# A GEGLU feed-forward block on one core: two raw products of the second column unit moved into the first one's second half, and the load queue of the down projection re-ordered

## The chip, the core and the metric

The kernel runs on one core of a Trainium2 chip. The metric is the device time in microseconds (us) of one execution; the lower, the better. Engines are named as in the profile: PE is the matrix engine, DVE the vector engine, ACT the scalar engine, POOL the GpSimd engine, SP the sync engine, which here only issues DMA transfers.

## What is computed

```python
B, S, Dm, Df = 1, 2048, 1024, 3584          # everything bf16
g = jnp.einsum("bsd,df->bsf", x, w_gate)
u = jnp.einsum("bsd,df->bsf", x, w_up)
h = jax.nn.gelu(g, approximate=True) * u
return jnp.einsum("bsf,fd->bsd", h, w_down)
```

## The kernel before

The 2048 rows of x are worked in two passes of 1024, each as two halves of 512 rows, `xT[0]` and `xT[1]`, held transposed. In a pass, the gate and up products come first, then the down projection.

**The gate and up products.** The 3584 hidden columns are cut into 14 units of 256 columns, each with one weight tile `w` of 2 x 512 KB (gate and up) from a pool of three buffers. A unit treats its product as a 2x2 block product and computes it in seven block products instead of eight, with sums of weight blocks (`s1` to `s4`, and `sa`, a cast) and sums of x blocks (`t1` to `t4`, and `tb`, a cast). The x sums serve the whole pass; a unit's weight sums are made a unit ahead on POOL. Each block product is 4 matmuls of 128x128 by 512 columns, and gate and up have one each, so a unit has 7 x 2 x 4 = 56 matmuls. Two of the seven use raw bf16 operands: `first_product` (L188), which needs only the weights' first half and `xT[0]`, and the product with `b21` at the head of `unit` (L205). The five others use the sums, in fp32r. A unit's order on PE is: `b21` product, s2 t2, s1 t1, s3 t3, s4 tb, then the next unit's `first_product`, then sa t4. Between s1 t1 and s3 t3 stands the call `after_p5()`, which is `prepare()` (L520): it makes the next unit's sums and issues loads.

Unit 0 of pass 0 is different: it has no sums and runs as plain products (`plain`, L471) of 32 matmuls for each half of x (a few of them cut in two). `xT[0]` is turned on PE. `xT[1]` comes by eight transposing DMAs on SP (L448), one for each block `ko` of 128 columns of x; the second half of unit 0 takes the blocks `ko` in order, two at a time.

**The down projection** (`down`, L361) is one large block product of the same kind with 14 column pairs j and a hand-written agenda. A step is a number in that agenda; on each step the functions due are called in the order they were entered, then `more(step)`, then the matmuls. Steps 0 to 27 use w_down as it is: 14 tiles `raw` of 256 KB, fetched by `fetch12`, each used by two steps of 4 matmuls. Then three stages follow that use sums of w_down blocks. Those sums are made in pass 0 (`keep_part`, `keep_whole`), stored to a DRAM tile `td` (`store_made`, L279, 768 KB each), and loaded again by `load12` (L286; for j = 0, 2 and 4 two at a time in 1 MB, with a buffer of the weight pool) and `load4` in both passes.

**What sets the order.** SP, DVE, POOL and PE run in the program's order throughout (`manual_schedule` with these engines). ACT is ordered by the compiler's own scheduler, except in blocks that add ACT to the list: the start with unit 0, and in unit 1 the snaps and the gelu after s2 t2. Small tiles come from one pool of 52 slots; an instruction that takes a slot waits for its last reader, and on SP everything behind it waits too. Weights of unit 1 and 2 are issued from ACT's queue, all later ones from SP's.

Of the kernel before, what the change touches and what calls it, by code (L numbers as in the profile page):

```python
# [1 line left out]

# [8 lines left out]
def kernel(  # L11
# [23 lines left out]
    nc = tc.nc  # L35
    ENG = mybir.EngineType
# [7 lines left out]
    ADD, SUB, MUL = ALU.add, ALU.subtract, ALU.mult  # L44
# [6 lines left out]
    NKB = Dm // P  # L51
# [8 lines left out]
    SLOTS = 52  # L60
    LAG = 3
    BIG12 = (0, 2, 4)
    AT12 = [2, 2, 5, 5, 8, 8, 16, 18, 20, 22, 27, 29, 31, 33]
    AT12S = [2 * j + (j > 8) for j in range(NJ)]
    AT73 = [30 + 2 * j if j < 8 else 46 + j - 8 for j in range(NJ)]

# [28 lines left out]
    def new(eng, a, b, op, name, shape=None, dtype=None):  # L95
        t = slot(shape or [P, N], dtype or f32r, name)
        eng(t, a, b, op)
        return t
# [6 lines left out]
    def snap(ps, name):  # L105
        t = slot([P, N], f32, name)
        nc.scalar.copy(out=t, in_=ps)  # L107
        return t
# [5 lines left out]

    def load_w(u, queue=nc.sync, pinned=False):
        f0 = u * 2 * P
        w = wpool.tile([P, 2, NKB, 2 * P], bf16, name="w")
        for i, src in enumerate((w_gate, w_up)):  # L120
            got = queue.dma_start(
                out=w[:, i],
                in_=src[:, f0 : f0 + 2 * P].rearrange("(ko ki) f -> ki ko f", ki=P),
            )
            if queue is not nc.sync and not pinned:
                tc.keep_in_program_order(got)
        return w

    class Sums(dict):
# [6 lines left out]
    def sums_t(xT):  # L136
        K = range(KH)
        lo, hi = [[xT[c][:, k] for k in K] for c in range(2)], [
            [xT[c][:, KH + k] for k in K] for c in range(2)
        ]  # L140
        return Sums(
            how={
                "t1": lambda q: [new(dve, lo[1][k], lo[0][k], SUB, "t1") for k in K],
                "t2": lambda q: [new(dve, hi[1][k], q["t1"][k], SUB, "t2") for k in K],
                "t3": lambda q: [new(dve, hi[1][k], lo[1][k], SUB, "t3") for k in K],
                "t4": lambda q: [new(dve, hi[0][k], q["t2"][k], SUB, "t4") for k in K],
                "tb": lambda q: [cast(hi[1][k], "tb") for k in K],
            }
        )
# [26 lines left out]
    def gelu(src):  # L176
        g = slot([P, N], f32, "g")
        nc.scalar.activation(g, src, ACT.Gelu_apprx_tanh)  # L178
        return g
# [4 lines left out]
    def product(ps, lhs, rhs, start):  # L184
        for k in range(KH):
            matmul(ps, lhs[:, k, :], rhs[k], start and k == 0, k == KH - 1)
# [6 lines left out]
    def unit(u, banks, xT, w, s, t, p1, after_p5, aside, keep, ahead_of_p4, snap_first):  # L193
        GU = range(2)

        def add(ps, other):

            g = new(dve, ps[0], other[0], ADD, "sum", dtype=f32)
            dve(ps[1], ps[1], other[1], ADD)
            return g, ps[1]  # L200

        b21 = [xT[0][:, KH + k, :] for k in range(KH)]
        e, c, d = banks
        aside(-1)
        for i in GU:  # L205
            product(c[i], w[:, i, KH:, :P], b21, True)
        g, up = add(c, p1)
        for i in GU:
            product(e[i], s["s2"][i], t["t2"], False)
        aside(0)  # L210
        keep(0, c[0])
        if snap_first:
            with tc.manual_schedule(engines={ENG.Activation}):
                u2 = [snap(e[i], "u2") for i in GU]
                g = gelu(g)
        else:
            g = gelu(g)
        times(2 * u, 0, g, up)
        if not snap_first:
            u2 = [snap(e[i], "u2") for i in GU]  # L220
        keep(1, c[0])
        keep(2, c[1])
        c = d
        for i in GU:
            product(c[i], s["s1"][i], t["t1"], True)
        p5 = [snap(c[i], "p5") for i in GU]
        after_p5()
        for i in GU:
            product(e[i], s["s3"][i], t["t3"], False)
        g, up = new(dve, e[0], p5[0], ADD, "sum", dtype=f32), banks[1][1]  # L230
        dve(up, e[1], p5[1], ADD)
        for i in GU:
            product(c[i], s["s4"][i], t["tb"], False)
        times(2 * u + 1, 1, gelu(g), up)
        aside(1)
        g, up = add(c, u2)
        ahead_of_p4()
        for i in GU:
            product(e[i], s["sa"][i], t["t4"], False)
        times(2 * u, 1, gelu(g), up)  # L240
        aside(2)
        times(2 * u + 1, 0, gelu(e[0]), e[1])
# [36 lines left out]
    def store_made(j):  # L279
        nc.sync.dma_start(out=td[:, j], in_=made[j][:, :3].bitcast(f32))  # L280
# [55 lines left out]
    def at(step, what, j):  # L336
        agenda.setdefault(int(step), []).append((what, j))

    for n in range(NJ):
        at(max(-1, 2 * n - 6), fetch12, n)  # L340
    for j in range(NJ):
        at(AT12[j], load12, j)
        at(AT12S[j], make12, j)
# [121 lines left out]
    wf = wpool.tile([P, 2, NKB, 2 * P], bf16, name="w")  # L465
    for k0, k1 in ((0, 2), (2, 5), (5, NKB)):
        load_wf(nc.sync, k0, k1)
    for ko in range(NKB):
        transposing(xT, 1, ko, N)

    def plain(ps, c, kos, parts=1):  # L471
# [14 lines left out]
    def finish(ps, c):  # L486
        for j in range(2):
            times(j, c, gelu(ps[2 * j]), ps[2 * j + 1])

    on_dve, on_act = nc.vector.tensor_copy, nc.scalar.copy  # L490
    t = sums_t(xT)
    with tc.manual_schedule(engines={ENG.Activation}):
        for _ in range(NWARM):
            nc.tensor.matmul(bank[3], lhsT=warm[:, :P], rhs=warm, start=True, stop=True)
        for i in range(NS):
            turn(xT, xn0, 0, i, on_act if i == 1 else on_dve)
        w = load_w(1, nc.scalar, pinned=True)
        s = sums_s(w, dve)
        plain(bank[0:4], 0, range(0, 2), parts=2)
        plain(bank[0:4], 0, range(2, NKB))  # L500
        t.make("t1")
        finish(bank[0:4], 0)
        s.make("s1", "s2")
        t.make("t2", "t3", "tb")
        s.make("s3", "sa")
        plain(bank[4:8], 1, range(NKB))
        finish(bank[4:8], 1)

    def making(u):
        if u < 2 or u >= NU:  # L510
            return []
        return list(range(u - 2, NJ if u == NU - 1 else u - 1))

    nxt = {}
    ahead = None
    for ip in range(NPASS):
        for u in range(1 if ip == 0 else 0, NU):
            js = making(u) if ip == 0 else []

            def prepare():  # L520
                nonlocal ahead
                nxt["w"], nxt["s"] = ahead, None
                if u + 1 < NU:
                    nxt["s"] = make_s(ahead, pool)
                if u + 2 < NU:
                    ahead = load_w(u + 2)
                if js:
                    store_made(js[0])
                for j in js[1:]:
                    keep_whole(j)  # L530
                if ip == 0:
                    fetch_wd(making(u + 1))

            def keep(part, ps):
                if js:
                    keep_part(js[0], part, ps)

            def aside(part):
                nonlocal ahead
                if ahead is None:  # L540
                    ahead = load_w(2, nc.scalar)
                if part == 0 and "s4" not in s:
                    s.make("s4")
                    t.make("t4")

            def ahead_of_p4():
                if u + 1 < NU:
                    nxt["p1"] = first_product(even if u % 2 else odd, xT, nxt["w"])

            e = odd if u % 2 else even  # L550
            p1 = nxt.pop("p1", None) or first_product(e, xT, w)
            unit(u, (e, cc, dd), xT, w, s, t, p1, prepare, aside, keep, ahead_of_p4, ip == 0 and u == 1)
            if u + 1 < NU:
                w, s = nxt["w"], nxt["s"]

        last = ip == NPASS - 1
        got, nxt = {}, {}

        def more(step):

            nonlocal ahead
            if last:
                return
            if step in (-1, 1):
                store_made(NJ - 2 + (step > 0))
            if step == 0:
                xT[:] = new_x()
            if step >= 16 and step % 2 == 0 and step // 2 - 8 < len(moves):
                c, ko = moves[step // 2 - 8]
                transposing(xT, c, ko, (2 * (ip + 1) + c) * N)  # L570
            if step == 50:
                got["w"], ahead = load_w(0), load_w(1)
            if step == 58:
                got["s"] = make_s(got["w"], dve)
            if step == 62:
                got["t"] = make_t(xT)

        down(ip, even + cc, dd + odd, last, more)
        even, odd, cc, dd = odd, even, dd, cc
        if not last:  # L580
            w, t, s = got["w"], got["t"], got["s"]
# [29 lines left out]
```

## Time and profile before

| | us |
|---|---|
| median of 5 runs (lowest to highest) | 548.98 (547.61 to 549.56) |
| the profiled execution's own time | 549.56 |
| its span | 547.7 |
| PE busy in the span | 535.4 (98%) |
| DVE, ACT, POOL busy | 341.4, 258.4, 237.2 |

The span is the time from the first to the last recorded instruction; 1.9 us of the profiled execution lie outside it. The profiled execution was 0.58 us above the median. PE's granted clock was 0.999 of full speed. In a timeline row, the two leading numbers are start and duration in us from the span's start, and the brackets at the end tell how long the engine had been idle and what ended that. A row of `SPq` or `ACTq` is a DMA being issued, not its transfer.

### The profile page before, as it was taken

The numbers are of one execution on the slowest core, as the hardware profiler recorded it, in microseconds if no ns is written. First come the engines' busy times: TensorE is split into PE (matmuls) and PEld (weight loads), VectorE is DVE, ScalarE is ACT, GpSimd is POOL, SyncE is SP. The second block draws the span as 40 slices with busy tenths as digits, with TensorE's granted clock in tenths as the row PEclk, the third lists the DMA queues.
The fourth block names the chain that finished last, engine by engine and source line by source line (L and its number), as shares of the span: only waits on it lengthen the run. The fifth ranks groups of instructions, "written<-read, shape, count | busy, mean of one in ns | idle before, by whom it ended". The sixth has DMA issues, their size and how long they took to land.

```text
span 547.7 us, 7414 instructions
## 1 busy us (share of the span) xinstructions
PE 535.4 (98%) x2405; PEld 377.6 (69%) x2405; DVE 341.4 (62%) x526; ACT 258.4 (47%) x463; POOL 237.2 (43%) x212
## 2 busy tenths in 40 slices
PE   8899999999999889999999999999999999999997
PEld 4377777767766635888877776776677775478885
DVE  3796666776677893495955555455555449766730
ACT  2466666656665410155445555555555551114531
POOL 0069976677774400000077677777777600000000
PEclk9999999999999999999999999999999999999999
DMA  8885666666655599999745222222222059463751
GB/s 206 154 215 174 174 174 187 208 182 196 201 162 172 204 387 284 295 230 262 279 127 142 79 78 77 78 77 78 77 78 77 1 182 376 152 230 95 222 192 49
DMA packets 108133, 93.28 MB, mean 170 GB/s; under 512 B 17216, under 2 KB 92992, under 8 KB 108096
## 3 DMA queue, kind: packets, MB, share of 16 engines
q1 hardware_dynamic: 103936, 90.72, 56.8%
q10 hardware_dynamic: 4160, 2.10, 1.5%
q8 instruction: 19, 0.31, 0.2%
q14 instruction: 18, 0.15, 0.1%
HBM read 74.45 MB, written 15.20 MB: 164 GB/s over the span
## 4 chain that ended last, share of the span: by engine, by line
PE 92%; DMA 5%; SPq 2%; issue 0%; ACT 0%
PE bank L111 92%; DMA raw<-in_w_down_dram 2%; DMA xT<-in_x_dram 2%; DMA td<-w 1%; SPq L448 1%; SPq L454 1%; SPq L329 0%; SPq L437 0%; ACT st L408 0%; SPq L290 0%; SPq L280 0%
## 5 line engine op out<-in xcount | busy, mean ns | idle before, releaser
L93 POOL TENSOR_TENSOR s<-w 128x512 fp32r<-128x512 bf16 x100 | 117.8, 1198 | 191.5 <-DVE t L90 92.8
L111 PE MATMUL bank<-t,s 128*128 128x512 f32 x648 | 157.0, 398 | 0.0
L111 PEld LDWEIGHTS bank<-t,s 128*128 128x128 f32 x648 | 121.7, 188 | 27.7
L111 PE MATMUL bank<-xT,w 128*128 128x512 bf16 (+1 forms) x504 | 116.7, 377 | 2.7 <-DMA xT<-in_x_dram 2.4
L107 ACT COPY p<-bank 128x512 f32<-128x512 f32 x124 | 70.5, 591 | 96.9 <-PE bank L111 96.9
L90 DVE TENSOR_TENSOR hT<-g,bank 128x512 bf16<-128x512 f32 x112 | 76.6, 687 | 53.8 <-ACT g L178 47.9
L111 PEld LDWEIGHTS <-w 128*128 128x128 bf16 x504 | 44.9, 98 | 62.4 <-issue 16.3
L90 DVE TENSOR_TENSOR sum<-bank,p 128x512 f32<-128x512 f32 x54 | 37.4, 692 | 53.2 <-PE bank L111 48.1
L178 ACT ACTIVATE g<-sum 128x512 f32<-128x512 f32 x81 | 51.5, 635 | 32.9 <-DVE sum L90 31.9
L111 PE MATMUL bank<-q 128*128 128x512 f32 x240 | 58.9, 389 | 0.0
L111 PE MATMUL bank<-t,sa 128*128 128x512 f32 x216 | 58.6, 413 | 0.0
L93 POOL TENSOR_TENSOR s<-w,s 128x512 fp32r<-128x512 bf16 x50 | 57.8, 1174 | 0.0
L93 POOL TENSOR_TENSOR s<-s,w 128x512 fp32r<-128x512 f32 x50 | 57.1, 1163 | 0.0
L111 PE MATMUL bank<-raw,hT 128*128 128x512 bf16 x224 | 49.2, 379 | 4.6 <-DMA raw<-in_w_down_dram 4.6
L111 PE MATMUL bank<-tb,s 128*128 128x512 f32 x216 | 53.3, 389 | 0.0
L111 PEld LDWEIGHTS bank<-q 128*128 128x128 f32 x240 | 45.0, 188 | 9.4
L111 PEld LDWEIGHTS bank<-t,sa 128*128 128x128 f32 x216 | 40.7, 188 | 10.6
L111 PEld LDWEIGHTS bank<-tb,s 128*128 128x128 f32 x216 | 40.5, 188 | 8.4
L102 ACT CAST tb<-raw 128x512 fp32r<-128x512 bf16 x28 | 17.2, 627 | 61.4 <-PE bank L111 26.1
L107 ACT COPY u<-bank 128x512 f32<-128x512 f32 x62 | 35.9, 590 | 20.1 <-PE bank L111 20.1
L111 PEld LDWEIGHTS <-hT 128*128 128x128 bf16 x224 | 21.8, 98 | 31.6 <-issue 6.0
L90 DVE TENSOR_TENSOR bank<-bank,p 128x512 f32<-128x512 f32 x54 | 37.8, 699 | 8.3 <-PE bank L111 5.1
(44 smaller groups left out, 457.1 us busy)
## 6 DMA issues: line engine op xcount, KB each, us to landing
raw<-in_w_down_dram SPq DMA_DIRECT2D x80, 256.0 KB, 4.8
q<-td SPq DMA_DIRECT2D x60, 256.0 KB, 5.2
w<-in_w_gate_dram SPq DMA_DIRECT2D x25, 512.0 KB, 4.7
w<-in_w_up_dram SPq DMA_DIRECT2D x25, 512.0 KB, 6.0
td<-m SPq DMA_DIRECT2D x12, 768.0 KB, 4.5
w<-td SPq DMA_DIRECT2D x6, 1024.0 KB, 9.1
out_dram<-st SPq DMA_DIRECT2D x32, 128.0 KB, 1.7
td<-w SPq DMA_DIRECT2D x2, 768.0 KB, 6.9
```

The source lines that it names most:

```text
L90: nc.vector.tensor_tensor(out=out, in0=a, in1=b, op=op)
L93: nc.gpsimd.tensor_tensor(out=out, in0=a, in1=b, op=op)
L102: nc.scalar.copy(out=t, in_=src)
L107: nc.scalar.copy(out=t, in_=ps)
L111: nc.tensor.matmul(ps, lhsT=lhs, rhs=rhs, start=start, stop=stop, skip_group_check=True)
L178: nc.scalar.activation(g, src, ACT.Gelu_apprx_tanh)
L448: nc.sync.dma_start_transpose(out=xT[c][:, ko, :], in_=x2[r0 : r0 + N, ko * P : (ko + 1) * P])
L454: got = queue.dma_start(out=wf[:, i, k0:k1], in_=src[k0 * P : k1 * P, 0 : 2 * P].rearrange("(ko ki) f -> ki ko f", ki=P),)
```

## The change

At the start, unit 1's weights are issued on SP between the fourth and the fifth transposing load, no longer on ACT. PE's order becomes: unit 0's second half for `ko` 0 to 3, unit 1's `first_product`, unit 1's `b21` product, unit 0's second half for `ko` 4 to 7, then unit 1's s2 t2. What unit 0 still has to do (`finish`, some sums) is called out of `unit` through `aside(-2)` and `aside(-1)`, and `t3` is made in two pieces around `finish`. The whole of unit 1 has ACT in program order. Unit 2's weights, on ACT's queue still, are issued in `prepare()` of unit 1, so behind the two p5 snaps, and no longer at the head of unit 1. In the down projection, `fetch12` comes two steps earlier, so four tiles are due at step -1 instead of three; the three 1 MB loads go from steps 2, 5, 8 to 6, 10, 14; the store of j = 11 goes from unit 13 to step -1 and those of 12 and 13 to steps 0 and 2, each behind that step's fetches; the transposing loads for pass 1 begin at step 24 instead of 16.

```diff
-    AT12 = [2, 2, 5, 5, 8, 8, 16, 18, 20, 22, 27, 29, 31, 33]
+    AT12 = [6, 6, 10, 10, 14, 14, 16, 18, 20, 22, 27, 29, 31, 33]
...
         e, c, d = banks
-        aside(-1)
         for i in GU:
             product(c[i], w[:, i, KH:, :P], b21, True)
+        aside(-2)
         g, up = add(c, p1)
+        aside(-1)
         for i in GU:
             product(e[i], s["s2"][i], t["t2"], False)
...
     for n in range(NJ):
-        at(max(-1, 2 * n - 6), fetch12, n)
+        at(max(-1, 2 * n - 8), fetch12, n)
...
-    for ko in range(NKB):
+    for ko in range(KH):
+        transposing(xT, 1, ko, N)
+    w = load_w(1)
+    for ko in range(KH, NKB):
         transposing(xT, 1, ko, N)
...
-        w = load_w(1, nc.scalar, pinned=True)
-        s = sums_s(w, dve)
         plain(bank[0:4], 0, range(0, 2), parts=2)
         plain(bank[0:4], 0, range(2, NKB))
         t.make("t1")
         finish(bank[0:4], 0)
+        plain(bank[4:8], 1, range(KH))
         s.make("s1", "s2")
-        t.make("t2", "t3", "tb")
-        s.make("s3", "sa")
-        plain(bank[4:8], 1, range(NKB))
-        finish(bank[4:8], 1)
+        nxt = {"p1": first_product(odd, xT, w)}
+
+    def rest_of_0(part):
+        if part == 0:
+            t.make("t2", "tb")
+            plain(bank[4:8], 1, range(KH, NKB))
+        else:
+            t3 = t["how"]["t3"](t, range(0, 2))
+            finish(bank[4:8], 1)
+            t["t3"] = t3 + t["how"]["t3"](t, range(2, KH))
+            s.make("s3", "sa")
...
             def prepare():
                 nonlocal ahead
+                if ahead is None:
+                    ahead = load_w(2, nc.scalar)
                 nxt["w"], nxt["s"] = ahead, None
                 if u + 1 < NU:
                     nxt["s"] = make_s(ahead, pool)
                 if u + 2 < NU:
                     ahead = load_w(u + 2)
-                if js:
+                if len(js) == 1:
                     store_made(js[0])
...
             def aside(part):
-                nonlocal ahead
-                if ahead is None:
-                    ahead = load_w(2, nc.scalar)
+                if (ip, u) == (0, 1) and part < 0:
+                    rest_of_0(part + 2)
...
-            unit(u, (e, cc, dd), xT, w, s, t, p1, prepare, aside, keep, ahead_of_p4, ip == 0 and u == 1)
+            first = (ip, u) == (0, 1)
+            with tc.manual_schedule(engines={ENG.Activation}) if first else nullcontext():
+                unit(u, (e, cc, dd), xT, w, s, t, p1, prepare, aside, keep, ahead_of_p4, first)
...
-            if step in (-1, 1):
-                store_made(NJ - 2 + (step > 0))
+            if step in (-1, 0, 2):
+                store_made({-1: NJ - 3, 0: NJ - 2, 2: NJ - 1}[step])
...
-            if step >= 16 and step % 2 == 0 and step // 2 - 8 < len(moves):
-                c, ko = moves[step // 2 - 8]
+            if step >= 24 and step % 2 == 0 and step // 2 - 12 < len(moves):
+                c, ko = moves[step // 2 - 12]
                 transposing(xT, c, ko, (2 * (ip + 1) + c) * N)
```

More of the change, by code (lines that the diff above doesn't have):

```diff
@@ L1 @@
-from contextlib import ExitStack
+from contextlib import ExitStack, nullcontext
 import concourse.bass as bass
@@ L113, in matmul, with load_w @@
         )
-    def load_w(u, queue=nc.sync, pinned=False):
+    def load_w(u, queue=nc.sync):
         f0 = u * 2 * P
@@ L120, in load_w @@
         for i, src in enumerate((w_gate, w_up)):
-            got = queue.dma_start(
+            queue.dma_start(
                 out=w[:, i],
@@ L124, in load_w @@
             )
-            if queue is not nc.sync and not pinned:
-                tc.keep_in_program_order(got)
         return w
@@ L144, in sums_t @@
                 "t2": lambda q: [new(dve, hi[1][k], q["t1"][k], SUB, "t2") for k in K],
-                "t3": lambda q: [new(dve, hi[1][k], lo[1][k], SUB, "t3") for k in K],
+                "t3": lambda q, K=K: [new(dve, hi[1][k], lo[1][k], SUB, "t3") for k in K],
                 "t4": lambda q: [new(dve, hi[0][k], q["t2"][k], SUB, "t4") for k in K],
@@ L212, in unit @@
         if snap_first:
-            with tc.manual_schedule(engines={ENG.Activation}):
-                u2 = [snap(e[i], "u2") for i in GU]
-                g = gelu(g)
+            u2 = [snap(e[i], "u2") for i in GU]
+            g = gelu(g)
         else:
@@ L490 @@
     on_dve, on_act = nc.vector.tensor_copy, nc.scalar.copy
-    t = sums_t(xT)
+    s, t = sums_s(w, dve), sums_t(xT)
     with tc.manual_schedule(engines={ENG.Activation}):
@@ L512, in making @@
         return list(range(u - 2, NJ if u == NU - 1 else u - 1))
-    nxt = {}
     ahead = None
```

## The prediction

> **What bounds the kernel now.** I read the page first: PE is busy for 535.4 of 547.7 us and never throttled, so a gain can only come from its idle 12.3 us. The list of waits by engine, cut to PE, says which idle time waits for something (columns: total us, times, longest):
>
> ```profile
> PE bank L111 <- DMA raw<-in_w_down_dram: 4.6, 4, 1.5
> PE bank L111 <- DMA xT<-in_x_dram: 2.4, 1, 2.4
> ```
>
> These 7.0 us are all that this change can win; the rest is 1.2 us at the start, 3.4 after the last matmul and two waits of 0.2. The PE timeline shows where they lie:
>
> ```profile
> 9.07 8.37 PE L111 MATMUL bank<-xT,w 128*128 128x512 bf16 x38 [0.25 <-DMA w<-in_w_up_dram]
> 19.88 7.11 PE L111 MATMUL bank<-xT,w 128*128 128x512 bf16 x32 [2.43 <-DMA xT<-in_x_dram]
> 26.63 5.84 PE L111 MATMUL bank<-t,s 128*128 128x512 f32 x24
> ...
> 34.12 1.90 PE L111 MATMUL bank<-xT,w 128*128 128x512 bf16 x8
> 35.67 2.19 PE L111 MATMUL bank<-t,sa 128*128 128x512 f32 x8
> ```
>
> At 17.45 PE has done unit 0 up to `ko` 3 of the second half and waits for the fifth transposing load; the matmuls at 34.12 are unit 2's `first_product`, the first work that needs unit 2's weights, and unit 1's sa t4 follows it at 35.67. The head of the first down projection:
>
> ```profile
> 188.84 8.79 PE L111 MATMUL bank<-raw,hT 128*128 128x512 bf16 x40 [1.54 <-DMA raw<-in_w_down_dram]
> 198.76 1.89 PE L111 MATMUL bank<-raw,hT 128*128 128x512 bf16 x8 [1.13 <-DMA raw<-in_w_down_dram]
> 202.08 3.61 PE L111 MATMUL bank<-raw,hT 128*128 128x512 bf16 x16 [1.43 <-DMA raw<-in_w_down_dram]
> 206.16 10.52 PE L111 MATMUL bank<-raw,hT 128*128 128x512 bf16 x48 [0.47 <-DMA raw<-in_w_down_dram]
> ```
>
> SP's timeline tells why: it held the first w_down tile behind a store that waited for its sums, and put 1 MB loads needed only at step 28 ahead of tiles needed at once.
>
> ```profile
> 182.76 0.33 SPq L280 DMA_DIRECT2D td<-m  x1
> 183.19 2.65 SPq L329 DMA_DIRECT2D raw<-in_w_down_dram  x3
> 185.93 0.42 SPq L280 DMA_DIRECT2D td<-w  x1
> ...
> 189.74 1.42 SPq L290 DMA_DIRECT2D w<-td  x1
> ```
>
> From 183 to 207 the DMA engines were full (the view by windows: share 1.00, 361 GB/s), so there order alone decides what is late. In the second pass, where nothing is stored, the same fetches started 15 us ahead of their stage (at 456.40) and PE didn't wait:
>
> ```profile
> 441.21 4.91 SPq L329 DMA_DIRECT2D raw<-in_w_down_dram  x5
> ```
>
> **The start.** Unit 1's two raw products are 16 bf16 matmuls. The 32 between 19.88 and 26.63 took 0.211 us each, so 16 are 3.4 us, more than the wait of 2.43; PE reaches `ko` 4 at 17.45 + 3.38 = 20.83. The two weight loads cost SP 0.38 and 0.58 us of issue (its rows at 23.56 and 23.98) and delay transposes 5 to 8 by 1.0 us; but the same bytes stood before them already: in before, the ACT loads issued at 10.83 and 11.33 landed after 4.9 and 8.4 us (the DMA view, one issue at a time), at 15.7 and 19.8, and transposes 5 to 8 at 19.8 to 20.8. In one queue the gate half lands at about 15.5 and the up half at 17.0, ahead of their uses at 17.5 and 18.3. At worst the up half comes at 19.8 again, a wait of 1.5. DVE's new order has each sum ready: t2 about 21.4 for 24.2, s3 about 27.6 for 28.0, s4 28.9 for 29.9 (operations at 0.62 from unit 0's last hT product at 25.1, by its rows of now); the 0.4 us at s3 is the thinnest margin. So s2 t2 starts at 24.2, 2.43 early. ACT loses two DMA issues from its start; it waited for PE there, so that is worth nothing.
>
> **The price.** Unit 2's weights now stand behind the p5 snaps. ACT's rows of before:
>
> ```profile
> 25.30 0.37 ACTq L121 DMA_DIRECT2D w<-in_w_gate_dram  x1
> 25.71 0.60 ACTq L121 DMA_DIRECT2D w<-in_w_up_dram  x1
> ...
> 32.61 0.62 ACT L102 CAST sa<-w 128x512 fp32r<-128x512 bf16 x1 [1.32 <-DMA w<-in_w_gate_dram]
> 34.37 0.62 ACT L102 CAST sa<-w 128x512 fp32r<-128x512 bf16 x1 [1.15 <-DMA w<-in_w_up_dram]
> ```
>
> They landed after 7.3 and 8.6 us, just in time for 34.12 + 0.78. The second p5 snap starts at about 30.7 now, so at 28.3 after; a DMA issues as the copy before it starts (25.29 and 25.30), so the halves go out at 28.3 and 28.75. PE wants them at 34.12 - 2.43 = 31.7. Bounds: an unhindered pair (SP's at 23.56) took 4.1 and 5.4 us, the pair above 7.3 and 8.6; up lands between 34.2 and 37.3. Ahead of it stand two 256 KB tiles, fewer than in before, but unit 4's pair now leaves SP at about 29.0, when s4 frees its buffer (31.46 in before), and shares the way. I take 34.5 for gate and 36.5 for up, nearer the crowded row. PE stands at `first_product` and starts sa t4 at 36.5 + 0.78 = 37.3 against 35.67: the start's 2.4 us are gone and **1.6 us more is lost**; the ends give -0.7 to +2.4, and +3.6 if unit 4's pair takes half the way throughout. Behind the loads, ACT also queues the two sa casts, then gelu, the next p1 snaps; all hang on the same landing: bank cc[1] is free 2.0 us after it, PE wants it 3.6 after; POOL's first s2 is done 2.3 after, wanted 4.4 after. So no second wait.
>
> Two rules bear on this price. By the Trainium skill's page "DMA: Bandwidth & Descriptors", section "Anatomy of one DMA", a DMA takes a fixed 2.0 us plus its bytes at 436 GB/s (fitted on GpSimd's path): 3.2 us for 512 KB, so gate at 31.5 and up at 32.0 to 32.7, no wait over 0.2 and a start of -2.2. The unhindered row, 4.1, already says longer. By its section "Queues, rings and completion order", each DMA engine takes turns between the queues, which speaks against the change: sharing with unit 4's pair, up would land at about 37.4 (estimate: 2.1 MB from 30.3 on, at about the 300 GB/s of before's 29.4 to 34.35). In order of issue, which the row w3-up (SP, 23.98, 5.4 us, not slowed by ACT's pair) looks like, it would be 35.3. My 36.5 lies between.
>
> **The down queue.** Needs: 48 matmuls from 206.16 took 0.212 each, so a w_down tile lasts 1.70 us, tile n is wanted at 187.2 + 1.70 n. Supply, from successive landings in the crowd: tile 0.70 us, td store 1.85, 1 MB load 2.6, q pair 1.4. After unit 12's fetches SP is free at 174.0; the second pass's row says the first four tiles' slots are then free, so they land by about 182. The store of j = 11 still goes at 182.76 (DVE) and lands at 188.15 as now. From there: tile 4 at 188.9 (wanted 194.0), 5 at 191.4, 6 at 193.9, 7 at 194.6, 8 at 197.9 (200.8), 10 at 201.9 (204.2), 12 at 205.9 (207.6), 13 at 208.0 (209.3). All four waits, 4.6 us, go, with 1.3 to spare at the end. Tile 9 had to wait in before for the slot of tile 4 (SP until 197.65); the same would hold it to 195.7 and cost 0.3 at tile 13. The first 1 MB load is wanted at 211 and lands near 197: moving them costs nothing. Later transposes: the last q of the P2 stage landed 3.7 us ahead (233.8 for 237.5); PE comes 4.6 sooner, but four transposes fewer stand ahead of it (1.1 us of SP each, 4.5). The last transposes land near 259, DVE reads them after 265: nothing.
>
> **Sum.** -4.6 + 1.6 = -3.0: 549.56 becomes 546.6 for an execution like the profiled one, 0.58 above the median, so **546.0** against 548.98. About 0.2% (1.1 us) is what a measurement tells from no change.
>
> **Rivals.** (a) Unit 2's weights land in time: -2.4 - 4.6 = -7.0, 542.0. The rule's 3.2 us speaks for it, every row of that transfer against. (b) The first four tiles can't go early, only just ahead of the store: 2.5 us of the queue's slack are used, waits of 1.3 remain, -3.3 + 1.6 = -1.7: 547.2. (c) Slower: SP stands at the fourth tile for a slot. Everything is behind it; from a restart at X, tile 13 lands at X + 25.65, so PE waits X - 183.65. If the slot is the first tile's own, freed at 188.9, that is 5.3 us in place of 4.6, with the start +2.3 us: 551.3. It is slower by over 0.2% from X = 187.8. For it: tile 9's wait above; against: five tiles in 4.91 us in the second pass. (d) Given back in the P2 stage: DMA share there is 1.12, so waits of 1 to 3 us could come on q: 547.0 to 549.0.
>
> **How the numbers follow.** Main case 0.58 (543.7 to 548.0); (a) 0.08, (b) 0.14, (c) 0.12, (d) 0.08. Faster: 0.55 of the main case, 0.08, 0.08 and 0.03, so 0.74; same: 0.03, 0.05, 0.03 and 0.02, so 0.13; slower 0.13, of which 0.10 from (c), the rest bad ends of (b) and (d). The range 543.6 to 549.2 leaves out (a) and most of (c).
>
> **What would show it.** Right: no wait at 17.45 and the 2.43 gone; a new PE wait for w_gate and w_up of some 4 us in total from 32 on (2.8 and 1.2); ACTq rows near 28.3; first w_down rows on SP before 180 and no PE wait for raw. Wrong: PE waiting for DVE near 28 (s3), SP idle before its fourth tile, or PE waits for q after 207.

## The result and the profile after

The changed kernel takes 547.18 us at the median (27 runs, 545.11 to 552.81) against 548.69 for the kernel before (48 runs): a ratio of 0.9973, 95% interval 0.9961 to 0.9984. It is faster, by 1.5 us; 546.0, a gain of 3.0, had been forecast. The profiled execution of the changed kernel has a span of 545.5 us.

PE's list of waits after (columns: total us, times, longest) no longer has either of the two waits of before. Waits for unit 2's weights stand in their place (0.57 us of the first row are unit 1's up half, at 18.31):

```profile
PE bank L111 <- DMA w<-in_w_up_dram: 2.1, 2, 1.5
PE bank L111 <- DMA w<-in_w_gate_dram: 1.5, 1, 1.5
```

PE's timeline after, at the start and at the head of the first down projection:

```profile
18.88 6.22 PE L111 MATMUL bank<-xT,w 128*128 128x512 bf16 x28 [0.57 <-DMA w<-in_w_up_dram]
24.74 6.04 PE L111 MATMUL bank<-t,s 128*128 128x512 f32 x24
30.63 1.97 PE L111 MATMUL bank<-tb,s 128*128 128x512 f32 x8
34.11 1.04 PE L111 MATMUL bank<-xT,w 128*128 128x512 bf16 x4 [1.51 <-DMA w<-in_w_gate_dram]
36.64 1.89 PE L111 MATMUL bank<-xT,w 128*128 128x512 bf16 x4 [1.49 <-DMA w<-in_w_up_dram]
37.97 2.93 PE L111 MATMUL bank<-t,sa 128*128 128x512 f32 x8
40.74 1.90 PE L111 MATMUL bank<-xT,w 128*128 128x512 bf16 x8
...
190.18 24.35 PE L111 MATMUL bank<-raw,hT 128*128 128x512 bf16 x112
```

The last row is the down projection's raw stage in one piece: 112 matmuls and no wait, where before four waits had cut it. The rows from 34.11 on are what the change costs: `first_product` of unit 2 comes in two halves, each behind a wait of 1.5 us, and unit 1's sa t4 starts at 37.97 where it had started at 35.67. ACT's timeline has the reason, unit 2's weights issued as the second p5 snap starts, and landing when the sa casts can run:

```profile
28.79 0.59 ACT L107 COPY p<-bank 128x512 f32<-128x512 f32 x1 [0.22 <-PE bank L111]
28.80 0.43 ACTq L121 DMA_DIRECT2D w<-in_w_gate_dram  x1
29.27 0.59 ACTq L121 DMA_DIRECT2D w<-in_w_up_dram  x1
34.09 0.62 ACT L102 CAST sa<-w 128x512 fp32r<-128x512 bf16 x1 [4.71 <-DMA w<-in_w_gate_dram]
36.62 0.62 ACT L102 CAST sa<-w 128x512 fp32r<-128x512 bf16 x1 [1.91 <-DMA w<-in_w_up_dram]
```

SP's timeline after shows the down queue as it was meant: four w_down tiles are out before the store of j = 11, which still waits for DVE's sum.

```profile
177.21 3.74 SPq L327 DMA_DIRECT2D raw<-in_w_down_dram  x4
185.81 0.34 SPq L278 DMA_DIRECT2D td<-m  x1
```

One more thing is in this profile that the prediction had not counted. The eight matmuls of sa t4 took 40.74 - 37.97 = 2.77 us against 2.03 before. The view by windows has PE's granted clock beside it (columns from the left: window, its length, each engine's busy us and instructions, then PEclk, the DMA share and GB/s):

```profile
34.00:36.00 2.00, 1.04 (x4) 0.31 (x4) 0.58 (x1) 0.62 (x1) 1.15 (x1) 1.00 1.20 290
36.00:38.00 2.00, 1.36 (x5) 0.54 (x5) 0.20 (x1) 1.38 (x3) 1.34 (x2) 0.53 1.20 290
38.00:40.00 2.00, 2.00 (x7) 1.61 (x6) 1.90 (x4) 1.43 (x3) 2.00 (x2) 0.62 0.30 71
40.00:42.00 2.00, 2.00 (x10) 0.98 (x10) 1.36 (x3) 0.60 (x1) 2.00 (x3) 1.00 0.00 0
```

In the trace's clock record PE has half its clock from 36.11 on, half a microsecond before the second wait ends, for 3.41 us. The windows agree: (1 - 0.53) x 2 + (1 - 0.62) x 2 = 1.7 us of clock are missing, which is half of 3.4. Between 38 and 40 only 7 matmuls start, between 40 and 42 ten. As an estimate from these rows, PE worked at half speed from 36.64 to 39.5 and lost some 1.4 us by it.

### The profile page after: what moved, and what is told of

Same layout as the page of the kernel before. It is cut to its first block, busy times and chain, and to the rows that moved or that the text cites. A ratio compares the mean times of both kernels' runs of the same rounds, so it can differ in the third digit from the quotient of the medians.

```text
span 545.5 us, 7422 instructions
## 1 busy us (share of the span) xinstructions
PE 536.9 (98%) x2405; PEld 378.4 (69%) x2405; DVE 341.9 (63%) x526; ACT 258.5 (47%) x463; POOL 236.9 (43%) x212
## 4 chain that ended last, share of the span: by engine, by line
PE 94%; DMA 3%; SPq 2%; ACT 0%; issue 0%
PE bank L111 94%; DMA w<-in_w_up_dram 3%; SPq L446 1%; SPq L452 1%; SPq L435 0%; ACT st L406 0%; SPq L121 0%; ACT p L107 0%
## 5 line engine op out<-in xcount | busy, mean ns | idle before, releaser
L90 DVE TENSOR_TENSOR q<-hT 128x512 fp32r<-128x512 bf16 x56 | 38.4, 686 | 4.3 <-PE bank L111 4.3
```

What stands on the lines that cost most here:

```text
L90: nc.vector.tensor_tensor(out=out, in0=a, in1=b, op=op)
```

## The experiments

Each kernel below is the changed kernel or the kernel before with the edit that is shown. Times are medians, beside runs of the kernel before on the same chip.

**The down queue alone.** The kernel before with the change's edits of `AT12`, `fetch12`, `store_made` and the first transposing step, and none of the start's.

```diff
-    AT12 = [2, 2, 5, 5, 8, 8, 16, ...
+    AT12 = [6, 6, 10, 10, 14, 14, 16, ...
-        at(max(-1, 2 * n - 6), fetch12, n)
+        at(max(-1, 2 * n - 8), fetch12, n)
...
-            if step in (-1, 1):
+            if step in (-1, 0, 2):
...
```

> The kernel before with the change's down queue alone (fetches two steps earlier, 1 MB loads, stores and pass 1's transposes later). My theory: the four waits for w_down tiles go, 4.6 us, so 544.1 and no PE wait for raw. Rival (part of it is given back later in the pass, or the waits had come from the start's shift): 545.5 to 547, with new PE waits behind 215.

Measured: 543.77 against 548.62, ratio 0.9911 (0.9897 to 0.9924), 4.9 us faster. The list of PE's waits has no w_down tile and no new wait later in the pass; behind the first 6 us only this is left:

```profile
PE bank L111 <- DMA xT<-in_x_dram: 0.7, 2, 0.4
```

So the down queue is worth its 4.6 us or a little more and gives nothing back, and it is faster by itself than together with the start's part.

**The start alone.** The changed kernel with the five edits of the down queue undone.

> The changed kernel with the down queue of before, so the start's part alone. My theory: the start costs 1.6 us in executions where PE's clock stays whole and 3 in those where it is halved behind the waits, so 550 to 552, slower than before by 0.2 to 0.5%; the waits for w_down tiles return, 4 to 5 us. Rival (the start is neutral, and the down queue gains less than 4.6): 548.5 to 549.

Measured: 553.84 against 548.62, ratio 1.0108 (1.0092 to 1.0124), 5.2 us slower and beyond the expectation. The profiled execution, at 550.69 the quickest, had PE's clock whole, although PE waits 1.7 us for the gate half and then 0.8 for the up half; 4.9 us more are waits for w_down tiles. The other four, 553.50 to 555.42, had a mean clock of 0.993, about twice the loss of a single halving (0.996). The 5.2 us are also more than what the start takes from the down queue alone (547.2 or 545.9, against 543.8). Where those executions' second halving stood was not profiled.

**Unit 2's weights early.** In the changed kernel they go out on SP behind the transposing loads.

```diff
     for ko in range(KH, NKB):
         transposing(xT, 1, ko, N)
+    ahead = load_w(2)
...
-                if ahead is None:
-                    ahead = load_w(2, nc.scalar)
```

> Only edit to the changed kernel: unit 2's weights go out on SP directly behind the transposing loads (issue near 19.6, landing before 26) in place of ACT's queue behind the p5 snaps. My theory (the start's price is the late landing of these weights, 3.0 us of PE waits, plus some 1.4 us of a halved PE clock just behind them): both go, PE starts unit 1's sa t4 near 33.6 in place of 37.97, no clock record of 0.5 near 36, time about 542 to 543. Rival 1 (another wait is hidden behind this one, DVE's sums or POOL's): PE waits for DVE or POOL near 31 to 38 and only 1 to 2 us are won. Rival 2 (nothing at the start matters, what was not won was lost in the down projection): no change, about 547.

Measured: 550.46 against 548.62, ratio 1.0037 (1.0025 to 1.005): slower than either kernel. The theory fell. The first rival had the cause right, but it had still allowed a gain of 1 to 2 us. PE's waits in this run:

```profile
PE bank L111 <- DVE s L90: 2.8, 1, 2.8
PE bank L111 <- DVE sum L90: 2.5, 1, 2.5
```

Behind each of the two the clock record is 0.5 for 3.41 us once more, from 31.69 and from 41.93. The weights had landed by 25.75, and POOL began unit 2's sums at 24.27, ten us earlier than in the changed kernel. At that time DVE was making its own sums from operands in SBUF. DVE's and POOL's rows of this run:

```profile
26.28 3.16 DVE L90 TENSOR_TENSOR t<-xT 128x512 fp32r<-128x512 bf16 x2
29.36 3.21 DVE L90 TENSOR_TENSOR s<-w 128x512 fp32r<-128x512 bf16 x2
32.48 3.21 DVE L90 TENSOR_TENSOR s<-w,s 128x512 fp32r<-128x512 bf16 x2
```

```profile
27.28 3.17 POOL L93 TENSOR_TENSOR s<-s,w 128x512 fp32r<-128x512 f32 x2
30.40 3.17 POOL L93 TENSOR_TENSOR s<-w 128x512 fp32r<-128x512 bf16 x2
```

Pairs that take DVE 1.28 and POOL 2.29 us when they run apart take 3.2 us on both, in step. The Trainium skill's page "SBUF — State Buffer", section "SBUF: two separate sides", describes a pair of ports that the two engines share: of a DVE operation with two inputs in SBUF and a GpSimd operation that reads SBUF, whichever starts first has it for the whole instruction, and the other stands still. Taking turns, one operation of each would need 0.64 + 1.15 = 1.8 us (an estimate from the rows of the engines apart); 1.6 were seen.

**Early weights, POOL held.** The same, but POOL first reads a corner of DVE's last t4.

```diff
                 nxt["w"], nxt["s"] = ahead, None
+                if (ip, u) == (0, 1):
+                    held = t["t4"][KH - 1][:, :64]
+                    new(pool, held, held, SUB, "held", [P, 64])
```

> Unit 2's weights on SP behind the transposing loads, as before in the run that came out slower, but POOL's first sum for unit 2 waits for DVE's last t4 (a small POOL subtraction reads it). Theory: what made the early weights slow was POOL working beside DVE on operands in SBUF (DVE's sums 1.65 us in place of 0.68, POOL's 1.6 in place of 1.15), not the weights' place. Then DVE is back at 0.68, PE waits for neither weights nor DVE, sa t4 starts near 33.6, time 541.7. Rival (the DVE order or SP's extra load itself is too slow): PE still waits 2 us or more near 28 to 40 and the time stays at 544 or above.

Measured: 542.80 against 548.77, ratio 0.9891 (0.9877 to 0.9906), 6 us faster than before, though 1.1 above the expectation. POOL's and DVE's rows:

```profile
32.84 0.29 POOL L93 TENSOR_TENSOR held<-t 128x64 fp32r<-128x64 f32 x1 [31.53 <-DVE t L90]
33.09 2.29 POOL L93 TENSOR_TENSOR s<-w 128x512 fp32r<-128x512 bf16 x2
```

```profile
26.65 1.28 DVE L90 TENSOR_TENSOR t<-xT 128x512 fp32r<-128x512 bf16 x2
27.86 1.28 DVE L90 TENSOR_TENSOR s<-w 128x512 fp32r<-128x512 bf16 x2
```

With the weights in the same place as in the run before, DVE's pairs are back at 1.28. PE's timeline and, behind the first 6 us, its list of waits:

```profile
34.01 2.17 PE L111 MATMUL bank<-t,sa 128*128 128x512 f32 x8
```

```profile
PE bank L111 <- DMA w<-in_w_up_dram: 0.3, 1, 0.3
```

The one wait left is for unit 1's up half. So the two engines' meeting was the cause there, and in the changed kernel the late weights had kept POOL away from DVE (it begins at 34.14 there), at a price. Beginning at 33.09, POOL's sums were still in time: PE's timeline has no wait for them.

**The weights ahead of the snaps.** Still on ACT's queue, but issued before the u2 snaps in `aside(0)` and not in `prepare()`.

```diff
             def prepare():
-                if ahead is None:
-                    ahead = load_w(2, nc.scalar)
...
             def aside(part):
...
+                if part == 0 and ahead is None:
+                    ahead = load_w(2, nc.scalar)
```

> The changed kernel with unit 2's weights still on ACT's queue, but ahead of the u2 snaps (issue near 26.2 in place of 28.8). Theory of the price: they land 2.6 us earlier at most, about 32 and 34.5, so PE's waits shrink from 3.0 to 1 us or less, no halved clock, POOL starts when DVE's t4 is nearly done; time 543.5 to 544.5. Rival (POOL's earlier start costs as much as the weights win): 546 to 547 with DVE sums over 1 us.

Measured: 543.57 against 548.77, ratio 0.9898 (0.9882 to 0.9914). It went as the theory of the price has it, though the issue came at 24.97 and not at 26.2: the up half landed at 33.9 and PE waited 0.15 us for it. POOL began in the middle of DVE's sums, and this time POOL alone lost:

```profile
29.23 5.94 POOL L93 TENSOR_TENSOR s<-w 128x512 fp32r<-128x512 bf16 x2 [27.93 <-DMA w<-in_w_gate_dram]
```

```profile
29.34 1.28 DVE L90 TENSOR_TENSOR s<-w,s 128x512 fp32r<-128x512 bf16 x2
30.55 2.49 DVE L90 TENSOR_TENSOR t<-xT,t 128x512 fp32r<-128x512 bf16 x4
```

POOL's first sum took 4.82 us and its second 1.16, while each of DVE's kept its 0.68. So a meeting of the two does not always slow both, and here PE had no wait from it.

**Fillers in the waits.** In the changed kernel PE gets 6 matmuls of zeros ahead of each half of unit 2's `first_product`; in a second kernel 4 and 2.

```diff
         for i in range(2):
+            for _ in range(fill[i]):
+                nc.tensor.matmul(e[i], lhsT=warm[:, :P], rhs=warm, start=True, stop=True)
```

> The changed kernel with 6 matmuls of zeros (0.21 us each, overwritten by what follows) ahead of each half of unit 2's first product, so PE works through most of its two waits of 1.5 us for these weights without being later. Theory of the clock (PE idle twice within 5 us has its clock halved for 3.4 us): no 0.5 record near 36, sa t4 takes 2.0 us and not 2.8, time about 545.4, and the executions scatter less. Rival (the slow matmuls near 37 come from the crowded DMA or from the weights, not from idle PE): same 547.2, or slower by the fillers where the weights land early.

> The fillers in PE's two waits cut from 6 and 6 to 4 and 2 matmuls, 1.3 us in place of 2.6. If the fillers had cost time where the weights came early, while keeping the clock whole was worth 1.4 us, this is 545.4 to 546.2 and still without a 0.5 record near 36. If the whole clock is worth nothing on the path, 547.

Measured: 547.01 (ratio 0.9971, 0.9959 to 0.9982) and 546.20 (0.9954, 0.9939 to 0.9968). All twelve executions of the two kernels had a mean clock of at least 0.999, where 18 of 28 executions of the changed kernel had 0.997 or less, with the same transfers. So PE's idle time is what halves the clock here. But the time that this should have won doesn't show: with 6 and 6 it is that of the changed kernel, and with 4 and 2 it is not below the 545.85 that the changed kernel takes in its second measurement (next), where five of six executions had the whole clock without fillers. Part of the fillers may stand in PE's way where the weights land early; this is not shown. Both profiled executions are the slowest of their six and have the weights late: PE still waits 0.9 and 2.2 us, and its s2 t2 starts at 25.96 and 25.62, against 24.74 in the changed kernel's profile. That delay is older than the fillers: PE's clock record reaches full speed only at 10.0 and 9.4 us, in the changed kernel's profile at 5.4. What the halved clock costs at the median is left open by these two.

**The changed kernel again**, with a second profile.

> The changed kernel once more, beside the others on one chip. Theory of the clock: its executions fall in two groups, about 545.4 with PE's clock whole and 547.5 with one record of 0.5 behind the waits for unit 2's weights; which one depends on how much of one 3.41 us stretch PE idles. Rival: the time scatters in one group and the clock has no part in it.

Measured: 545.85 against 548.77, ratio 0.9948 (0.9932 to 0.9963). The one execution with a clock of 0.996 took 547.18, the five with at least 0.999 took 545.05 to 546.39. In the first 27 runs and the profiled one the same holds: ten with at least 0.999 lie between 545.11 and 546.31, eighteen with 0.997 or less between 546.55 and 552.81. This profile is one with the whole clock:

```profile
33.72 1.04 PE L111 MATMUL bank<-xT,w 128*128 128x512 bf16 x4 [1.50 <-DMA w<-in_w_gate_dram]
35.51 1.04 PE L111 MATMUL bank<-xT,w 128*128 128x512 bf16 x4 [0.75 <-DMA w<-in_w_up_dram]
36.20 2.20 PE L111 MATMUL bank<-t,sa 128*128 128x512 f32 x8
38.24 1.90 PE L111 MATMUL bank<-xT,w 128*128 128x512 bf16 x8
```

From s2 t2 (24.38) to the row after sa t4 it takes 13.86 us, where the first profile took 40.74 - 24.74 = 16.00. Of the 2.14 us between them, 0.75 are waits (3.00 against 2.25) and about 1.4 slower matmuls. In these two profiles the longer waits and the fallen clock come together, so the 2 us between the groups are not the clock's alone. What decides to which group an execution goes is not shown: 18 of 28 fell in the first measurement, 1 of 6 in this one.

**The kernel before again.** The same code, profiled a second time.

> The kernel before, profiled a second time. Theory: PE's wait of 2.43 us for the fifth transposing load is not the same in every execution (in the run with the down queue alone it was 0.69 in two pieces, with the same code at the start), so this profile shows 0.7 to 2.4 there, the four waits for w_down tiles near 4.6 us again, and 547.5 to 549.5. Rival: 2.43 again within 0.2, and the run with the down queue alone had moved it.

Measured: 548.58, ratio 1.0002 (0.9989 to 1.0016), and its waits for w_down tiles are 4.5 us. For the transposing loads, though, PE does not wait at all:

```profile
7.11 18.35 PE L111 MATMUL bank<-xT,w 128*128 128x256 bf16 x86
25.12 5.83 PE L111 MATMUL bank<-t,s 128*128 128x512 f32 x24
```

The first row runs from the first plain matmul to s2 t2 without a gap. The fifth transposing load, for which PE stood waiting in the first profile, landed at 17.80, where it had been 19.83. PE also came to it later, at about 18.4 and not 17.45 (an estimate: 32 matmuls of 0.211 us before 25.12). So the 2.43 us are no fixed cost of the program: that execution was the slowest of its five, and with the same start the down queue alone showed 0.7 in one profile and 0.6 in the next.

**The two best side by side**, and one more step, with PE doing both gate products of unit 1 ahead of both up products, on top of the held version:

```diff
-        for i in GU:
+        for i in GU if not snap_first else ():
             product(c[i], w[:, i, KH:, :P], b21, True)
...
-        nxt = {"p1": first_product(odd, xT, w)}
+        for i in range(2):
+            product(odd[i], w[:, i, :KH, :P], [xT[0][:, k, :] for k in range(KH)], True)
+            product(cc[i], w[:, i, KH:, :P], [xT[0][:, KH + k, :] for k in range(KH)], True)
+        nxt = {"p1": [snap(odd[i], "p1") for i in range(2)]}
```

> The kernel before with the down queue alone, once more, to stand beside the held version on one chip: 543.8, and PE's wait for the transposing loads between 0.7 and 2.4.

> The changed kernel with unit 2's weights early and POOL held until DVE's last t4, once more: 542.8. Theory (the start's part is worth about 1 us once its price is gone): 0.7 to 1.5 us below the down queue alone. Rival (it is worth nothing even then): the same time within 0.5.

> The held version with PE doing both gate products of unit 1 before both up products, so that the up half of its weights is wanted 0.85 us later. Theory: the wait of 0.3 to 0.6 us for that half near 18 goes, time 542.3. Rival (the transposing loads are wanted no later, so the wait moves to them): 542.8.

Measured, against 548.88: down queue alone 543.46 (0.9908, 0.9892 to 0.9924), held version 542.63 (0.9896, 0.988 to 0.9913), gate products first 542.45 (0.9889, 0.9874 to 0.9904). The held version is 0.8 us below the down queue alone here and was 1.0 below it in the earlier runs, which stood on different chips. The order is the same both times, but the intervals overlap, so this gain is likely and not certain. The last step's profile has no wait at 18 any more, but neither has the second profile of the held version, which lacks the step. PE's rows of the held version and of the last step:

```profile
7.68 18.70 PE L111 MATMUL bank<-xT,w 128*128 128x256 bf16 x86
```

```profile
7.69 18.36 PE L111 MATMUL bank<-xT,w 128*128 128x256 bf16 x86
```

In both, PE's clock record reaches full speed only at 10.2 and 9.6 us, so PE came late to those weights in any case; in the held version's first profile it was 5.4, and the wait stood at 18.54. What the step does to the wait is therefore not shown, and its gain of 0.2 us is below what these runs can tell. It has the lowest median found, 6.4 us below the kernel before.

## Why the prediction was right, and what was off

The sign, and a time within the range, came from the account's largest term: the waits in the down projection go, and they pay for a new wait at the start. The sum was -3.0; -1.5 was measured at first and -2.9 in the second measurement. The terms of the start were off, and in part against each other: its gain was much smaller than forecast, and so was the wait that pays for it, while the fallen clock was not foreseen. That -2.9 comes so near to -3.0 is in part luck.

- **The down queue, -4.6.** Right: all four waits gone, 4.9 and 5.4 us at the median with the edit alone. The first four tiles went out from 177.21 to 180.95, not quite unhindered: SP stood 1.9 us for a slot at the second of them, and for four more at later tiles. The slack took that, the more so as PE came to its first tile at 190.2; the prediction's 187.2 had left its own 1.6 us of price out. Rival (c), SP stuck at the fourth tile, did not happen, and neither did (b) or (d): PE has no wait for `raw` or `q` at any later time. (The -1.7 of (b) gives 547.3, not 547.2.)
- **The landing of unit 2's weights.** Right in mechanism and nearly in size. Issue at 28.80 and 29.27 (28.3 and 28.75 had been forecast), landing at 34.07 and 36.59 (34.5 and 36.5). PE's wait was 3.0 us and not 4.0, since PE came later to it. These two took 5.3 and 7.3 us with the DMA engines full (share 1.20 from 34 to 38), far from the 3.2 us of the prediction's first rule. No second wait came for cc[1] or POOL's s2.
- **The start's gain, -2.4: this term was mis-sized.** It was read off one execution. A second profile of the same kernel has 0 in its place, and the start's part is worth 0.8 to 1.0 us, with overlapping intervals, where its price has been removed (held version against the down queue alone). The wait at 17.45 was no fixed cost of the program.
- **The price, +1.6 beyond the start's gain.** In the profile after, the row behind sa t4 starts at 40.74, and before it had started at 37.70: 3.0 us later, not 1.6. By the medians the start took 3.4 us from the down queue alone in the first comparison and 2.1 to 2.4 in the second. The waits are 2.3 to 3.0 of it; what the prediction lacked is PE's halved clock behind them, some 1.4 us in the profile that has it.
- **Unit 1's up half** was to land at 17.0 and landed at 18.83: a wait of 0.57, inside the bound of 1.5. DVE's s3, the thinnest margin, was in time by then.
- **Rival (a)**, the weights in time, was said to give 542.0. It gives 542.8 where POOL is kept off DVE; the weights alone in time gave 550.5, and the prediction had nothing of it: it had asked of POOL only whether it would be late, not what it would slow by being early.

## What to carry to other kernels

A wait that is seen in one profile may be that execution's own: look at the scatter of the times, or at a second profile, before it goes into a sum, above all at the start where many transfers race. A transfer that is moved earlier also moves the engine that works on its data; ask which engine that one then meets. And on PE a wait of 2.5 us, or two shorter ones close together, can cost more than its length.

## What the runs showed of the hardware

- PE's clock was halved for 3.41 us behind two waits of 1.5 us with 0.8 us of matmuls between them (the profile after), and behind single waits of 2.8 and 2.5 us (unit 2's weights early). One wait of 1.54 us (w_down, before), two of 1.5 and 0.75 (the changed kernel again) and two of 1.7 and 0.8 (the start alone) left it whole, so the length of the waits alone does not decide. The Trainium skill's page "TensorE: Matmul & The Clock Gate", section "What's actually happening", has a free-running window of some 3.4 us in which PE's activity decides, which would fit that the same program gets the half clock in some executions and not in others. Its table has the clock fall after an idle window; here 3.0 idle us out of 4.0, in two pieces, were enough.
- When PE's clock becomes full at the start varies between executions of one program: at 5.4 and at 10.2 us in the two profiles of the held version. Between 7 and 10 us, 25 matmuls start in the first and 20 in the second.
- DVE and POOL sums with all operands in SBUF, run at the same time, took 1.6 us each in place of 0.68 and 1.15 where the two went in step; where POOL came into a row of DVE's sums, DVE lost nothing and POOL's sum took 4.82.
- In two executions of one program the fifth of the eight transposing loads at the start landed 2.0 us apart (19.83 and 17.80), the last 0.5 (20.84 and 20.30).
